# Fewer filler matmuls, a quartered first turn and an earlier weight load at the start of a fused Fourier filter and PReLU product kernel

## The chip, the cores and the metric

The kernel runs on one core of one Trainium2 chip. The metric is device microseconds of one execution; lower is better. The engines are TensorE (PE, whose weight loads are listed as PEld), VectorE (DVE), ScalarE (ACT), GpSimd (POOL) and SyncE (SP). SP and POOL issue the transfers.

## The reference

A Fourier filter along the sequence, then two products with a PReLU between them. There are 8 batches of 3008 tokens with 256 channels; the hidden width is 2048.

```python
def _attn_ref(x, filt_r, filt_i):
    X = np.fft.rfft(x, axis=1)
    F = (filt_r + 1j * filt_i)[None, :, :]
    Y = X * F
    return np.fft.irfft(Y, n=x.shape[1], axis=1).astype(np.float32)

def _moe_ref(x, w_in, w_out, alpha):
    h = x @ w_in
    g = np.maximum(h, 0.0) + alpha * np.minimum(h, 0.0)
    return (g @ w_out).astype(np.float32)
```

## The kernel before

The transform of length 3008 is split as 94 x 32. For a batch it has four steps on PE: a first stage of length 94 (`piece_a`), a stage of length 32 with twiddles (`piece_b`), the product with the filter on DVE, the inverse of length 32 (`piece_c`), and the inverse of length 94 (`inverse`, called by `half_d` and `pair_d`, L291), which leaves the filtered tokens transposed in `yT`. Between stages the data are turned. Batches 1 to 7 turn through DRAM while the products of earlier batches run. Batch 0 has nothing to hide behind, so class `First` turns it by matmuls with an identity.

After that the tokens go through in blocks of up to 512. A block's up-product (`up`, or `up4` for the very first block, L582) multiplies 16 slices of `w_in` with `yT`, ACT evicts, DVE computes the PReLU as g + min(g, 0) (alpha - 1), and the down-product (`down`, L613) multiplies with `w_out`. The first block's up-product is made in halves of 256 tokens: steps 0, 2, 4 and 6 take tokens 0 to 255, steps 8 to 14 the others. Work of the transforms is put between steps by hand with `put(step, ...)`. Every engine works its own list in the order in which the program wrote it.

What the change touches is all before step 2 of the first block:

- The first stage of batch 0 (loop at L459, pieces 0 to 7, two for each of the four loaded chunks of x). Between pieces `warm(n, ...)` (L455) puts n filler matmuls of 512 columns whose results nobody reads.
- The product loop (L493, kp = 0 to 11): `piece_b(kp + 2)` writes a product on DVE (L371), `piece_c(kp)` the inverse on PE (L392), `keep_c` the eviction. `piece_c` reads two tables, `twi_s` and its swapped copy `twx_s`; for kp = 4 to 7 the swapped copy is made by POOL (`swapped(8, nc.gpsimd)`, L445 and L446). At kp = 4 a memset on DVE (L497) and then the loads of `w_in` (L499), a chunk of x for batch 1, `w_out` (L502) and three more chunks of x are written into POOL's queue.
- The turn and the last stage of batch 0 (L519 to L524). `side_t(f)` turns the first four of 32 columns for channel half f, evicted by ACT for f = 0 and by DVE for f = 1. `half_t(2)` and `half_t(3)` turn two columns each of the next four. `half_d(0)` and `half_d(2)` make the last stage of the first 376 tokens for channel half 0 and 1.
- Step 0 evicts those two `half_t` and turns the PReLU slopes (`slopes`, L661 to L663); step 1 makes `half_d(1)` and `half_d(3)`, the next 376 tokens, and turns the next columns (`piece_t(2)`).

Accumulators: `bank("h")` takes one of two wide buffers (`psH`), `bank("f")` the single wide buffer `psF`, `bank("o")` one of two narrow ones (`psO`, 512 values). Buffers of a pool are used in turn, and a matmul into one waits for the eviction of what was in it.

Of the kernel before, what the change touches and what calls it, by code (L numbers as in the profile page):

```python
# [14 lines left out]
N1 = 94  # L15
# [40 lines left out]
def kernel(  # L56
# [10 lines left out]
    nc = tc.nc  # L67
# [37 lines left out]
    id16 = ids[:, 0:128]  # L105
# [4 lines left out]
    yT = konst.tile([128, 2, 2 * NFFT], FP16, name="yT")  # L110
# [5 lines left out]
    def load_x(b, c, held=False):  # L116
        xs = p_x.tile([128, 8 * D], FP16, name="xs")
        if held:
            for r in (slice(0, 32), slice(64, 96)):
                nc.vector.memset(xs[r, 0:2], 0.0)  # L120
        if b:
            for r in (slice(0, 48), slice(48, N1)):
                nc.gpsimd.dma_start(out=xs[r], in_=xrow(b, c)[r])  # L123
        else:
            w = 8 * D // (1 + (c == 3))
            for o in range(0, 8 * D, w):
                nc.gpsimd.dma_start(out=xs[0:N1, o : o + w], in_=xrow(b, c)[:, o : o + w])
        return xs
# [23 lines left out]
    def banks(wide):  # L152
        if wide:
            return psH.tile([128, 2, 512], FP32, name="hps")
        return psF.tile([128, 2, 512], FP32, name="psF")

    def bank(kind):
        if kind == "o":
            return psO.tile([128, 2, D], FP32, name="op").rearrange("p k d -> p (k d)")
        return banks(kind == "h")[:, 0]  # L160
# [151 lines left out]
    def on_act(o, i):  # L312
        nc.scalar.activation(o, i, AF.Copy)  # L313

    def on_dve(o, i):
        nc.vector.tensor_copy(o, i)  # L316

    both = (on_act, on_dve)


    class First(Fft):
# [86 lines left out]
                    nc.tensor.matmul(pt[0:96, u // 2, o : o + 128], m[:, f, n * i + u], id16,  # L408
                                     start=True, stop=True)

        def side_t(self, f):
            pt = bank("o")
            for u in range(4):
                nc.tensor.matmul(pt[0:96, 128 * u : 128 * u + 128],
                                 self.vm.rearrange("p (f s m) -> p f s m", f=2, m=96)[:, f, u], id16,
                                 start=True, stop=True)
            return self.zt[:, 0:4, 128 * f : 128 * f + 128], pt[0:96].rearrange("p (s d) -> p s d", s=4)

        def half_t(self, i, kind):
            pt = bank(kind).unsqueeze(1)  # L420
            self.turn(pt, i, 2)
            return self.zt[:, 2 * i : 2 * i + 2].rearrange("p a d -> p (a d)"), pt[0:96, 0]

        def piece_t(self, i, evict):
            pt = banks(False)
            self.turn(pt, i, 4)
            evict(self.zt[:, 4 * i : 4 * i + 4].rearrange("p (h a) d -> p h (a d)", h=2), pt[0:96])

    nc.sync.dma_start(out=ids, in_=id_d.ap())
    nc.vector.tensor_copy(signs_s, ids[:, 128:130])  # L430
# [2 lines left out]
    def table(ka, kb):  # L433
        nc.sync.dma_start(out=twf_s[:, ka:kb], in_=consts["twf"].ap()[:, ka:kb])

    def inverse_table(ka, pb):
        for i in range(4):
            nc.tensor.matmul(pb[:, 128 * i : 128 * i + 128],
                             twf_s[:, ka + 2 * i : ka + 2 * i + 2].rearrange("p k m -> p (k m)"), id16,
                             start=True, stop=True)  # L440
        on_act(twi_s[:, ka : ka + 8].rearrange("p k m -> p (k m)"), pb)

    def swapped(ka, eng):
        t, o = twi_s[:, ka : ka + 8], twx_s[:, ka : ka + 8]
        eng.tensor_scalar(o[:, :, 32:64], t[:, :, 0:32], gs_s, None, OP.mult)  # L445
        eng.tensor_scalar(o[:, :, 0:32], t[:, :, 32:64], gs_s, -1.0, OP.mult, OP.mult)  # L446

    xc = {(0, c): load_x(0, c) for c in range(4)}
    f0 = First()
# [3 lines left out]
    def warm(n, pw):  # L453
        for _ in range(n):
            nc.tensor.matmul(pw.rearrange("p (r c) -> p r c", r=4), id16,  # L455
                             id16.unsqueeze(1).to_broadcast([128, 4, 128]), start=True, stop=True)

    warm(10, bank("o"))
    for i in range(8):  # L459
        f0.piece_a(i, i % 3 < 2)  # L460
        if i == 3:
            inverse_table(0, bank("o"))
            swapped(0, nc.vector)
            warm(3, bank("o"))
        elif i % 2 == 1:
            warm((8, 0, 3, 0)[i // 2], bank("o"))
        if i in (5, 7):
            ka = 4 * i - 12
            nc.vector.memset(twf_s[:, ka : ka + 8, 0:1], 0.0)
            table(ka, ka + 8)  # L470
# [22 lines left out]
    for kp in range(12):  # L493
        if 0 < kp < 10:
            f0.piece_b(kp + 2)
        if kp == 4:
            nc.vector.memset(win_s[:, :, 0:1], 0.0)  # L497
            for kt in range(2):
                nc.gpsimd.dma_start(out=win_s[:, kt], in_=moe_w_in[kt * 128 : (kt + 1) * 128])  # L499
            xc[(1, 0)] = load_x(1, 0)  # L500
            for q in range(2):
                nc.gpsimd.dma_start(  # L502
                    out=wout_s[:, 8 * q : 8 * q + 8],
                    in_=moe_w_out[1024 * q : 1024 * q + 1024].rearrange("(j p) d -> p j d", p=128))
            for c in range(1, 4):
                xc[(1, c)] = load_x(1, c)
        f0.piece_c(kp)
        if kp > 9:
            f0.keep_c(kp, (on_act, on_act) if kp == 10 else both, 1)
        elif kp % 2 == 1:  # L510
            f0.keep_c(kp - 1, (on_act, on_act))
            if kp < 7:
                f0.turn_at(kp + 5, 2, on_act)
# [3 lines left out]
    for o in (32, 96):  # L517
        nc.gpsimd.dma_start(out=filt_s[o : o + 32], in_=filt_s[o - 32 : o])
    warm(3, bank("h"))  # L519
    on_act(*f0.side_t(0))  # L520
    on_dve(*f0.side_t(1))
    later = [f0.half_t(2, "h"), f0.half_t(3, "f")]
    f0.half_d(0, on_act, "o")
    f0.half_d(2, on_dve, "o")  # L524

    sizes = [512] * 5 + [384] + [512] * 6
    blocks = []
# [96 lines left out]
    def put(step, fn, *args):  # L624
        plan.setdefault(step, []).append((fn, args))
# [33 lines left out]
    def slopes():  # L659
# [2 lines left out]
        nc.vector.tensor_copy(al_s, alp[:, 0:16])  # L662
        nc.vector.tensor_scalar(alm_s, al_s, 1.0, -1.0, OP.mult, OP.add)  # L663

    put(1, f0.half_d, 1, on_act, "o")
    put(1, f0.half_d, 3, on_dve, "o")
    put(1, f0.piece_t, 2, on_dve)
# [22 lines left out]
    for b in range(3, NB):  # L690
        p = 96 * (b - 1)
# [20 lines left out]
    for step in range(16):  # L712
        if step % 2 == 0:
            blk.up4(step // 2 % 4, step // 8,
                    {0: [lambda: on_dve(*later[0]), lambda: on_act(*later[1]), slopes],
                     8: [lambda: f0.pair_d(3, on_dve)]}.get(step, []))
        for fn, args in plan.pop(step, ()):
            fn(*args)
# [4 lines left out]
    for p, t0, tn in blocks[1:]:  # L723
        blk = Block(p, t0, tn)
        for j in range(16):
            n = psum.get(step, 0)
# [50 lines left out]
```

## Time and profile before

| what | value |
|---|---|
| median of 3 runs | 769.6 us (769.01 to 769.75) |
| the profiled execution | 769.81 us, span 768.0 us |
| PE busy | 757.2 us (99% of the span) |
| DVE busy | 633.5 us (82%) |
| ACT busy | 582.8 us (76%) |
| POOL busy | 145.7 us (19%) |
| mean granted TensorE clock | 1.000 |

A stretch or a row gives its start and its length in microseconds from the span's start. In the timeline, brackets give the idle time of the engine before the row and what ended it. In the chain of waits each row is the work, the transfer or the wait that the next one had to wait for; "issue" is time in which nothing that the profile shows was waited for. In the table by stretches the columns are length, then busy time (and count) of PE, PEld, DVE, ACT and POOL, granted clock, the DMA engines' share and GB/s. Busy time of a matmul contains its passage through the array, so consecutive matmuls overlap.

### The profile page before, as it was taken

Reading aid. Unit: us, or ns where it says so; the run is one execution under the profiler, and the core shown is the slowest. Engines: PE = TensorE matmul, PEld = TensorE weight load, DVE = VectorE, ACT = ScalarE, POOL = GpSimd, SP = SyncE. Lnnn points to the kernel's source line nnn. Section 1 sums busy time; section 2 is a strip of 40 time slices with the busy share of each in tenths; the row PEclk is TensorE's granted clock in tenths of the full one; section 3 lists DMA queues with packets and bytes.
Section 4 is the critical chain, followed back from the end, with each engine's and each line's share of the span. In section 5 each row is a group of like instructions: output and inputs, shape, how many; then the busy total and the mean of one; then the engine's idle time right before and its main releaser. Section 6 shows DMA issues by size and latency. Waiting matters only on the chain.

```text
span 768.0 us, 16563 instructions
## 1 busy us (share of the span) xinstructions
PE 757.2 (99%) x6536; PEld 507.5 (66%) x6536; DVE 633.5 (82%) x1160; ACT 582.8 (76%) x670; POOL 145.7 (19%) x275
## 2 busy tenths in 40 slices
PE   8899999999999999999999999999999999999998
PEld 4666667666666666666666666766666666766666
DVE  4898975889889998899978998999877888666663
ACT  4787787888778787887778787787777777776664
POOL 6511560222211211121202222022101212000000
PEclk9999999999999999999999999999999999999999
DMA  9996796574853559533883538544453223510111
GB/s 163 168 237 166 148 200 200 155 175 128 189 144 78 137 136 199 147 93 95 186 212 87 134 94 180 177 93 118 129 158 92 71 68 96 152 36 28 42 42 56
DMA packets 97198, 100.04 MB, mean 130 GB/s; under 512 B 12054, under 2 KB 83366, under 8 KB 96928
## 3 DMA queue, kind: packets, MB, share of 16 engines
q1 hardware_dynamic: 82384, 69.50, 31.2%
q0 software_dynamic: 14736, 29.49, 21.3%
q8 instruction: 51, 0.84, 0.5%
q14 instruction: 27, 0.22, 0.1%
HBM read 55.02 MB, written 46.66 MB: 132 GB/s over the span
## 4 chain that ended last, share of the span: by engine, by line
PE 94%; DVE 2%; ACT 2%; DMA 1%; issue 0%; POOL 0%; ACTq 0%
PE op L613 42%; PE hps L559 41%; PE psF L291 3%; PE hps L269 2%; PE psF L238 1%; DMA win_s<-in_moe_w_in_dram 1%; PE op L455 1%; PE hps L184 1%; PE hps L210 1%; DVE gtb L596 1%; ACT asb L313 1%; DVE m L595 1%; PE hps L582 0%; ACT gtb L568 0%; DVE zt L316 0%
## 5 line engine op out<-in xcount | busy, mean ns | idle before, releaser
L568 ACT ACTIVATE gtb<-hps 128x1024 f16<-128x1024 f32 (+1 forms) x376 | 377.6, 1007 | 134.2 <-PE hps L559 131.1
L613 PE MATMUL op<-wout_s,gtb 128*128 128x256 f16 x3008 | 431.3, 273 | 0.0
L559 PE MATMUL hps<-yT,win_s 128*128 128x512 f16 (+1 forms) x1504 | 418.4, 375 | 0.9 <-ACT asb L313 0.3
L613 PEld LDWEIGHTS <-gtb 128*128 128x128 f16 x3008 | 290.8, 98 | 164.3 <-issue 10.7
L571 DVE TENSOR_SCALAR m<-gtb,alm_s 128x512 f16<-128x512 f16 (+1 forms) x752 | 227.0, 345 | 99.8 <-ACT gtb L568 98.3
L573 DVE TENSOR_TENSOR gtb<-gtb,m 128x2048 f16<-128x2048 f16 (+1 forms) x188 | 226.1, 1203 | 10.3
L559 PEld LDWEIGHTS <-win_s 128*128 128x128 f16 x1504 | 142.4, 98 | 55.2 <-issue 6.0
L252 POOL DMA_DIRECT2D sw<-ww x144 | 71.7, 506 | 414.5 <-DVE ww L245 408.7
L618 ACT ACTIVATE osb<-op 128x512 f32<-128x512 f32 (+1 forms) x97 | 56.6, 583 | 12.3 <-PE op L613 11.2
L313 ACT ACTIVATE asb<-hps 128x1024 f16<-128x1024 f32 (+1 forms) x56 | 56.6, 1019 | 5.6 <-PE hps L184 4.3
L313 ACT ACTIVATE v<-hps 128x1024 f16<-128x1024 f32 (+1 forms) x43 | 43.4, 1010 | 10.9 <-PE hps L269 10.6
L245 DVE TENSOR_TENSOR ww<-psF,filts_s 128x1024 f16<-128x1024 f32 x42 | 51.1, 1216 | 0.2 <-PE psF L238 0.2
L246 DVE TENSOR_TENSOR uu<-psF,filt_s 128x1024 f16<-128x1024 f32 x42 | 50.9, 1213 | 0.0
L313 ACT ACTIVATE yT<-psF 128x752 f16<-128x752 f32 x58 | 46.1, 795 | 2.0 <-PE psF L291 1.9
L291 PEld LDWEIGHTS <-zt 96*128 96x128 f16 x512 | 28.5, 98 | 6.8 <-issue 1.0
L291 PE MATMUL psF<-wi_s,zt 96*128 96x94 f16 x448 | 27.9, 205 | 0.1
L250 POOL DMA_DIRECT2D uu<-ww x24 | 19.7, 1232 | 31.8 <-DVE uu L246 23.8
L257 DVE TENSOR_TENSOR uu<-uu,sw 128x1024 f16<-128x1024 f16 x36 | 24.5, 681 | 0.3 <-DMA sw<-ww 0.3
L194 DVE TENSOR_TENSOR xs<-xs 47x2048 f16<-47x2048 f16 x16 | 19.5, 1219 | 0.4
L123 POOL DMA_DIRECT2D xs<-in_x_dram x24 | 17.5, 1012 | 12.2 <-PE hps L559 4.8
L198 DVE TENSOR_TENSOR xs<-xs 47x2048 f16<-47x2048 f16 x16 | 19.3, 1209 | 0.0
L269 PE MATMUL hps<-uu,twi_s 64*64 64x256 f16 x336 | 17.3, 281 | 0.0
(93 smaller groups left out, 261.5 us busy)
## 6 DMA issues: line engine op xcount, KB each, us to landing
out_dram<-osb SPq DMA_DIRECT2D x128, 128.0 KB
v_dram<-v SPq DMA_DIRECT2D x84, 128.0 KB
zt<-v_dram SPq DMA_DIRECT2D x28, 384.0 KB
sw<-ww POOLq DMA_DIRECT2D x144, 64.0 KB, 2.5
xs<-in_x_dram POOLq DMA_DIRECT2D x40, 192.0 KB, 6.3
at<-a_dram SPq DMA_DIRECT2D x40, 192.0 KB
a_dram<-asb SPq DMA_DIRECT2D x32, 192.0 KB
a_dram<-asb SPq DMA_DIRECT2D x12, 384.0 KB
```

The lines of the kernel that those rows point to most:

```text
L245: nc.vector.tensor_mul(ww, px, fs)
L246: nc.vector.tensor_mul(uu, px, f)
L252: nc.gpsimd.dma_start(out=sw[o : o + 32], in_=ww[i : i + 32])
L269: nc.tensor.matmul(ps[64 * par : 64 * par + 64, e, 256 * h : 256 * h + 256], twi_s[r, 4 * q + 2 * h + par], u[r, par, h], start=True, stop ...
L291: nc.tensor.matmul(ps[:, m], self.zt[:, 8 * g + 4 * mh + m, dh * 128 : dh * 128 + 128], self.wi, start=True, stop=True)
L313: nc.scalar.activation(o, i, AF.Copy)
L559: nc.tensor.matmul(self.hps[:, j % 2, 0:tn], win_s[:, kt, j * 128 : (j + 1) * 128], yT[:, kt, self.t0 : self.t0 + tn], start=(kt == 0), st ...
L568: nc.scalar.activation(g[:, 2 * i : 2 * i + 2], self.hps[:, :, 0:tn], AF.Copy)
L571: nc.vector.tensor_scalar(m[:, 2 * i + h], g[:, 2 * i + h], 0.0, a, OP.min, OP.mult)
L573: nc.vector.tensor_add(g, g, m)
L613: nc.tensor.matmul(self.op[:, si - s0], self.gts[k][:, 128 * si : 128 * si + 128], wout_s[:, k], start=(si == s0 and k == 0), stop=(si == ...
L618: nc.scalar.activation(osb[:, 0:m], self.op[:, 0:m], AF.Copy)
```

## The change

Four edits:

1. Fillers between first-stage pieces: 8, 0, 3, 0 after pieces 1, 3, 5, 7 become 4 after piece 1 and 1 after piece 5; the three after piece 3 stay.
2. `side_t` is replaced by `quarter_t(f, h, kind)`: two of the four columns each, h = 0 evicted by ACT and h = 1 by DVE, for f = 0 in narrow buffers and for f = 1 in wide ones. The next four columns are turned at once (`whole_t(1)`) into `psF` and evicted by DVE alone in step 0.
3. `half_d(0)` and `half_d(2)` are replaced by `first_d`, which makes only columns 0 to 63 of the last stage, which are tokens 0 to 255: channel half 0 in two parts of 32 columns (ACT and DVE), channel half 1 in one of 64 (ACT). The other 30 columns of both channel halves are made in step 1, in one narrow buffer evicted by ACT, ahead of `half_d(1)`.
4. The memset of `win_s` and the loads behind it move from kp = 4 to kp = 3.

```diff
-        def side_t(self, f):
-            pt = bank("o")
-            for u in range(4):
-                nc.tensor.matmul(pt[0:96, 128 * u : 128 * u + 128],
-                                 self.vm.rearrange("p (f s m) -> p f s m", f=2, m=96)[:, f, u], id16,
-                                 start=True, stop=True)
-            return self.zt[:, 0:4, 128 * f : 128 * f + 128], pt[0:96].rearrange("p (s d) -> p s d", s=4)
+        def quarter_t(self, f, h, kind):
+            pt = bank(kind)[0:96, 0:256].rearrange("p (s d) -> p s d", s=2)
+            for u in range(2):
+                nc.tensor.matmul(pt[:, u], self.vm.rearrange("p (f s m) -> p f s m", f=2, m=96)[:, f, 2 * h + u],
+                                 id16, start=True, stop=True)
+            return self.zt[:, 2 * h : 2 * h + 2, 128 * f : 128 * f + 128], pt
+
+        def first_d(self, dhs, x0, x1, kind):
+            n, w = len(dhs), x1 - x0
+            ps = bank(kind)[:, 0 : 4 * n * w].rearrange("p (a m x) -> p a m x", a=n, m=4)
+            for a, dh in enumerate(dhs):
+                for m in range(4):
+                    nc.tensor.matmul(ps[:, a, m], self.zt[:, m, 128 * dh : 128 * dh + 128], self.wi[:, x0:x1],
+                                     start=True, stop=True)
+            o = yT[:, dhs[0] : dhs[0] + n, 4 * x0 : 4 * x1]
+            return o.rearrange("p a (x m) -> p a x m", m=4), ps.rearrange("p a m x -> p a x m")
...
-        def piece_t(self, i, evict):
+        def whole_t(self, i):
             pt = banks(False)
             self.turn(pt, i, 4)
-            evict(self.zt[:, 4 * i : 4 * i + 4].rearrange("p (h a) d -> p h (a d)", h=2), pt[0:96])
+            return self.zt[:, 4 * i : 4 * i + 4].rearrange("p (h a) d -> p h (a d)", h=2), pt[0:96]
+
+        def piece_t(self, i, evict):
+            evict(*self.whole_t(i))
...
-        elif i % 2 == 1:
-            warm((8, 0, 3, 0)[i // 2], bank("o"))
+        elif i in (1, 5):
+            warm(4 if i == 1 else 1, bank("o"))
...
-        if kp == 4:
+        if kp == 3:
             nc.vector.memset(win_s[:, :, 0:1], 0.0)
...
     warm(3, bank("h"))
-    on_act(*f0.side_t(0))
-    on_dve(*f0.side_t(1))
-    later = [f0.half_t(2, "h"), f0.half_t(3, "f")]
-    f0.half_d(0, on_act, "o")
-    f0.half_d(2, on_dve, "o")
+    for f, kind in enumerate("oh"):
+        for h in range(2):
+            both[h](*f0.quarter_t(f, h, kind))
+    later = f0.whole_t(1)
+    on_act(*f0.first_d((0,), 0, 32, "o"))
+    on_dve(*f0.first_d((0,), 32, 64, "o"))
+    on_act(*f0.first_d((1,), 0, 64, "h"))
...
+    put(1, lambda: on_act(*f0.first_d((0, 1), 64, N1, "o")))
     put(1, f0.half_d, 1, on_act, "o")
...
-                    {0: [lambda: on_dve(*later[0]), lambda: on_act(*later[1]), slopes],
+                    {0: [lambda: on_dve(*later), slopes],
```

## The prediction

> **What bounds the kernel now.** I read the page's slices first, then the table by stretches, the chain of waits, and the timeline of the first 56 us, where every edit lies.
>
> ```profile
> PE   8899999999999999999999999999999999999998
> 56.00:256.00 200.00, 199.36 (x1636) 130.36 (x1633) 167.66 (x307) 160.13 (x182) 49.27 (x82) 1.00 0.65 160
> 256.00:456.00 200.00, 199.85 (x1687) 133.82 (x1686) 182.22 (x324) 159.04 (x182) 35.92 (x72) 1.00 0.54 134
> ```
>
> The second column of a stretch is PE's busy time: from 56 us on it idles 0.64 us, then 0.15 us, in 200. Nothing there is edited, so the change is worth what it moves the point at which this full stretch begins. Before it, by the chain:
>
> ```profile
> 24.41 0.43 POOL win_s L499
> 24.85 0.19 issue
> 25.03 8.59 DMA win_s<-in_moe_w_in_dram
> 33.62 0.05 issue
> 33.67 0.61 PE hps L582 x4
> ...
> 38.92 0.95 DVE yT L316
> ...
> 41.31 1.14 DVE m L595 x4
> ...
> 54.63 1.14 DVE zt L316
> 55.77 0.04 issue
> 55.82 0.49 PE psF L291 x8
> ```
>
> The second half of the first up-product (L582, kt = 1) waits for w_in until 33.67. PE then works without a gap to 39.82, its product at 38.39 releases DVE, and DVE is the chain from 40.45 to 55.77. So whatever is late at 35.32, where the second up-product starts, is late at 56. The edits act on two stretches ahead of it: first-stage pieces to products (6 to 30 us), and the turn (30 to 35).
>
> **The change, part by part.** All terms are against the profiled execution: span 768.0 us, 769.81 with what lies around it, 0.2 us above the median of 769.6 of three runs, so I add the difference to the median.
>
> *Fillers.* Six of 512 columns go: four after pieces 0 and 1, two after 4 and 5. Eight of them take 1.77 us in the chain, so 0.22 us each, 1.3 us off PE. Pieces 2 and 3 start at 9.85, their chunk has landed at 8.16 (trace's landings); they move up 0.88. The last half chunk lands at 11.89, so piece 7 (13.12) can move 1.0 at most; DVE casts without a gap from 12.29 to 14.35, and that row starts 0.85 sooner. So the first product (15.91) comes at about 15.05: its filter rows have landed at 14.72.
>
> What is late next is POOL.
>
> ```profile
> 22.33 0.49 POOL L446 TENSOR_SCALAR gtb<-twi_s,signs_s 128x256 f16<-128x256 f16 x1
> 22.55 0.10 PEld L392 LDWEIGHTS <-uu 64*128 64x128 f16 x2 [0.20 <-issue]
> 22.90 0.27 PEld L392 LDWEIGHTS <-uu 64*128 64x128 f16 x14 [0.25 <-issue]
> ```
>
> The fifth last-stage product (L392) stops after two matmuls until POOL has written its swapped table, 22.33 + 0.49 = 22.82. In the built order that matmul waits for POOL's semaphore. POOL's time doesn't depend on PE: it issues filter loads back to back from 18.77, which itself waited 0.37 us for a filter landing. So PE resumes at 22.9 as before, and from there to 25.33 it has no gap: the ninth product's input (L366, 24.45, 0.41 long) cannot be ready before 24.86, DVE follows 0.07 later (15.84 to 15.91 at the first), so at 24.93 instead of 25.15. Of 0.85 us, 0.22 is left. Bounds: the two table loads and five small ones on SP's queue, behind DVE's memsets, also go 0.85 sooner and share the DMA engines with the filter loads for which POOL waits; that could hold POOL up by one wait of the size seen (0.37), leaving -0.15. If POOL is somehow earlier, the next limit is the second third of the filter, landed at 19.78 for a product at 20.60: 0.75. I take 0.1, nearer the row.
>
> *Weights one product sooner.* The memset of w_in (0.06 us on DVE) stands behind the sixth product instead of the seventh, at about 22.1. POOL is free of its cast at 22.96, so it issues w_in there instead of at 24.41, and behind it, in unchanged order, the two loads of x, two of w_out and six more of x: all 1.44 sooner, past nothing else in POOL's queue. The second half lands at 33.62 less 1.44 if the engines give that time back; they are at 0.61 share in 24 to 28 us, and the two last table loads land only at 24.93, so I allow 0.2: 32.4. If the cover fails and only the idle share is won, (1 - 0.61) x 1.44 = 0.6: 33.0.
>
> *Quarters, and 256 tokens only.* Without a wait for weights, before: DVE's yT of the second half (32.64 + 0.55) would release kt = 1 at about 33.29. After, times before the 0.1 of the fillers: turning matmuls from 30.86, 0.056 apart; eviction starts 0.256 after the last matmul of its group (31.034 to 31.290). ACT's first quarter 31.18 to 31.57, DVE's 31.29 to 31.72, ACT's second 31.44 to 31.83, DVE's 31.64 to 32.06 (nearest rows: 256 wide, 0.384 on ACT, 0.425 on DVE, which overlap their successors by about 0.1). First-half products of 32 columns end for ACT at 32.15, for DVE at 32.32. The trace has no eviction of 128 values: between DVE's 16 wide copy (0.175) and its 256 wide cast (0.425); I take 0.29. So 32.61, and kt = 0 starts at 32.67, lasts four times 0.109, kt = 1 at 33.11; the second half (ACT, 256 wide) is ready at 32.87, w_in at 32.4, both hidden. 33.67 - 33.11 = 0.56 sooner, 0.66 with the fillers.
>
> *What is left over comes back behind it.* The remaining 30 columns of both halves become a new ACT eviction (240 values, between 0.384 for 256 and less; I take 0.37) and it stands behind the first activation of 1024 values:
>
> ```profile
> 34.37 1.02 ACT L590 ACTIVATE gtb<-hps 128x1024 f16<-128x1024 f32 x1 [1.09 <-issue]
> 35.29 0.48 ACT L313 ACTIVATE yT<-op 128x376 f16<-128x376 f32 x1
> ...
> 34.21 0.23 PE L661 MATMUL op<-id,al 16*128 16x16 f32 x1
> 34.37 0.66 PE L291 MATMUL op<-wif_s,zt 96*128 96x94 f16 x8
> 34.87 0.61 PE L408 MATMUL psF<-ids,v 128*96 128x128 f16 x8
> 35.32 1.04 PE L582 MATMUL hps<-yT,win_s 128*128 128x256 f16 x8
> ```
>
> Here PE runs from the up-product through both half products (L291) and the next turn to the second up-product, 33.67 to 35.32: 1.65 us. There are two small accumulator buffers ("o"). In the new sequence they go: slopes, the 30 columns, half product 1, half product 3. The last takes the buffer of the 30 columns, and the built order gives it a wait for ACT that it lacked. From the start of kt = 1: last matmul 0.33, activation starts 0.33 later, ACT's next 0.92 behind it (34.37 to 35.29), 0.37 for the eviction, 0.05 to the matmul, four matmuls 0.17, eight turns 0.45: 2.62. Behind the waiting matmul stand that turn and the second up-product, for which ACT, then DVE wait. Added: 2.62 - 1.65 = 0.97. Bounds: 0 if the eviction got ahead of the activation; 1.2 if it lasts as the 376 wide one (0.48) and the activation starts late as in the row at 36.39 plus 0.1. The single whole turn on DVE (1.21, for 0.68 there and 0.58 on ACT) ends at about 33.8, before half product 1 needs it at 34.1; it stays hidden.
>
> **Sum.** -0.56 - 0.1 + 0.97 = +0.3 us: 769.9.
>
> **Rivals.** (a) *The new wait costs nothing*: -0.66, 768.9; with the fillers' other bound of 0.75 in place of 0.1, 768.3. For: ACT has idle time at 34. Against: engines run in order and the eviction stands behind the activation. (b) *POOL doesn't hold the products*: +0.97 - 0.56 - 0.75 = -0.34, 769.3. (c) *The weights come no sooner*, because the transfers in front set their pace: kt = 1 at 33.67, +0.97, 770.6; for it, DMA engines at 1.08 share in 31 to 34; against, 0.61 in 24 to 28. (d) *The clock falls, slower*: the fillers keep TensorE fed while it waits for chunks. The first ten take 0.445 us each (4.45 in the chain), later ones 0.22, so PE starts at half rate, though the clock column says 1.00. If the gaps after 12.6 put it back for a stretch like the first one (2.5 to 8 us), half of 5.5 us of work is lost, 2.75, less PE's idle time there (0.16 + 0.3) and the 0.65 that POOL hides anyway: 1.6 on top of 0.3, 771.5. It decides from gaps longer than those that PE survives now, 0.72 us (29.09 to 29.81); I expect 0.2 to 0.6 us.
>
> The Trainium skill speaks on (d): "TensorE: Matmul & The Clock Gate", part 1, has the clock fall back after an idle window of about 3.4 us. The doubling of the fillers' rate agrees with its two states; that gaps of 0.72 us leave the rate alone agrees too, so by its rule (d) would not happen here.
>
> **Chances.** The forecast 0.42, (a) 0.18, (b) 0.12, (c) 0.11, (d) 0.10, something unseen 0.07. About 0.2%, 1.54 us, is what a measurement of this kernel can tell: faster means under 768.06, reached only by a third of (a) and a bit of the unseen: 0.07. Slower is over 771.14: (d), a quarter of (c) with the upper bound of the wait, and half of the unseen: 0.16. Within: 0.77. The range 768.5 to 771.2 takes in (a), (b), (c) and the unknown costs, and leaves out most of (d). The forecast's own range is 769.4 to 770.6.
>
> **What would show it.** Right: first product (DVE, filter row) at about 15.1, but the twelfth ending within 0.3 of 29.76; PE stopping at 22.9 for POOL; w_in's issue near 23.0 and no wait of L582's successor for it; kt = 1 near 33.0; the 240 wide eviction behind the first activation, an idle PE of about 0.8 us before the second half product, and the second up-product at 35.5 to 35.8. Wrong: that product before 35.2, the products' end before 29.3, or matmul durations doubled after 9 us. The forecast fails as a whole if the start of the full stretch at 56 doesn't carry over to the end.

## The result and the profile after

The changed kernel takes 771.74 us (median of 12 executions, 770.12 to 775.3); beside it on the same chip the kernel before takes 769.68 us (12 executions, 768.98 to 771.3). The ratio is 1.003 with an interval of 1.0016 to 1.0043: slower by 0.3%, where 769.9 was predicted and 771.2 was the upper end of the range.

The profiled execution took 772.23 us, 2.42 us more than that of before. The first view is its chain of waits (start, length, work).

```profile
12.32 1.53 POOL filt_s L147 x3
13.85 2.79 DMA filt_s<-in_filt_i_dram
16.64 1.23 DVE uu L371
...
30.91 1.40 PE hps L467 x3
32.30 0.43 PE op L414 x4
...
34.70 1.05 PE hps L596 x8
...
35.82 0.72 ACT gtb L604
36.54 0.20 issue
36.74 0.37 ACT yT L313
...
57.05 1.14 DVE zt L316
58.19 0.04 issue
58.23 0.49 PE psF L291 x8
```

The full stretch begins at 58.23 instead of 55.82, so all of the loss, 2.41 us, arises in the edited part. Two things in this chain were not in that of before. Loads of the filter (filt_s) hold DVE until 16.64. (The chain infers which load it was and names one issued at 13.85. The last load of the rows that this product reads is the one issued at 12.32; it landed at 16.21, and the product starts 0.42 us behind it, as it does 0.41 behind the same load in e1 and e5.) And the three fillers ahead of the turn (L467) take 1.40 us in the chain. From the first of them to the turn it is 1.25 us (30.84 to 32.09), where the same three took 0.71 in the trace of before (30.15 to 30.86): TensorE works at about half its rate. The table by stretches, in the columns explained with the profile before, has the clock; first the kernel before, then the changed one.

```profile
16.00:20.00 4.00, 3.54 (x107) 2.49 (x104) 4.00 (x4) 3.01 (x4) 3.55 (x8) 1.00 1.11 169
28.00:31.00 3.00, 2.05 (x63) 1.25 (x55) 2.18 (x3) 2.02 (x5) 2.08 (x4) 1.00 1.04 201
31.00:34.00 3.00, 2.51 (x31) 1.81 (x30) 1.83 (x3) 1.56 (x3) 0.10 (x1) 1.00 1.08 199
```

```profile
16.00:20.00 4.00, 2.40 (x77) 1.64 (x78) 3.37 (x3) 2.00 (x4) 3.49 (x8) 1.00 1.07 151
28.00:31.00 3.00, 2.13 (x80) 1.51 (x80) 2.35 (x4) 1.17 (x3) 1.51 (x3) 0.95 1.05 205
31.00:34.00 3.00, 3.00 (x25) 2.21 (x24) 1.22 (x3) 1.50 (x5) 0.81 (x2) 0.50 1.15 196
56.00:256.00 200.00, 199.20 (x1635) 130.28 (x1634) 168.23 (x307) 160.02 (x183) 47.61 (x79) 1.00 0.65 158
```

From 16 to 20 us PE is busy for 2.40 us instead of 3.54: this is the wait for the filter. From 31 to 34 the granted clock (third column from the end) is 0.50, and PE is busy throughout. The clock's own records put the half rate at 30.70 to 34.11 us, 3.41 us long. Over a span of 770 us one such stretch lowers the mean clock by 0.5 x 3.41 / 770 = 0.002, so the mean clock of an execution tells how many it had: 1.000 none, about 0.998 one, 0.996 two. (A last 0.001 more or less is the clock falling behind the last matmul, a little before the span ends; e12's fell at 767.19 of 767.81 us.) Of the 12 executions after, 2 had none (770.12 and 770.21), 6 had about one (median 771.6), 4 had two (median 773.6). The kernel before is not free of it: in the three groups in which it ran beside the experiments, 16 of 35, 15 of 35 and 17 of 33 executions were at 0.998 or less, and those at 1.000 had medians of 769.74, 770.04 and 769.50, those at 0.998 of 771.33, 771.12 and 770.90. One stretch costs it 1.1 to 1.6 us.

Why the filter came late shows in the timeline (start, length, engine, line, work, count, idle before). Before:

```profile
13.22 0.07 DVE L469 MEMSET twf_s<- 128x8 f16 x1
13.31 1.42 SPq L434 DMA_DIRECT2D twf_s<-c_twf  x2
15.91 2.35 DVE L371 TENSOR_TENSOR uu<-hps,filt_s 128x1024 f16<-128x1024 f32 x2 [0.21 <-DMA filt_s<-in_filt_r_dram]
```

After:

```profile
11.93 0.07 DVE L481 MEMSET twf_s<- 128x8 f16 x1
12.02 1.57 SPq L446 DMA_DIRECT2D twf_s<-c_twf  x2
12.32 0.49 POOL L147 DMA_DIRECT2D filt_s<-in_filt_i_dram  x1 [0.56 <-DMA xs<-in_x_dram]
16.63 2.36 DVE L371 TENSOR_TENSOR uu<-hps,filt_s 128x1024 f16<-128x1024 f32 x2 [2.08 <-DMA filt_s<-in_filt_i_dram]
17.91 0.30 PE L366 MATMUL hps<-at,twf_s 64*32 64x256 f16 x8 [1.44 <-DVE uu L371]
```

DVE's memset of the table twf_s comes 1.29 us sooner, because the casts ahead of it follow the first-stage pieces. SP's load of that table waits for the memset and is now issued at 12.02, ahead of the filter load that POOL issues at 12.32; before, it was issued at 13.31, behind the same filter load (12.17). By the landings in the trace this filter load landed at 14.72 before and lands at 16.21 after. DVE then idles 2.08 us and PE 1.44.

All fourteen profiles, those of the experiments below included, order themselves this way. In the six with few fillers and the tables not held back (after, e1, e6, e10, e11, e12) the table load is issued 0.02 to 0.35 us ahead of the filter load, which lands 3.5 to 4.0 us after its own issue. In the other eight it is issued 0.3 to 1.5 us behind, and the filter load lands 2.5 to 2.9 us after its issue.

Some 0.4 of the 1.29 us is not the fillers' doing. TensorE starts at half rate, and in the profiled execution its clock first rose at 6.81 us, in that of before at 8.20, so pieces 0 and 1 took 0.69 us instead of 1.28. In e10, where it rose at 8.03, the table load is issued at 12.42, 0.89 sooner than before, and still just ahead of the filter load (12.44).

### The profile page after: what moved, and what is told of

It reads as the page before. It is cut to its first block, busy times and chain, and to the rows that moved or that the text cites. A ratio compares the mean times of both kernels' runs of the same rounds, so it can differ in the third digit from the quotient of the medians.

```text
span 770.5 us, 16579 instructions
## 1 busy us (share of the span) xinstructions
PE 757.1 (98%) x6542; PEld 507.6 (66%) x6542; DVE 633.8 (82%) x1161; ACT 582.7 (76%) x672; POOL 145.1 (19%) x275
## 4 chain that ended last, share of the span: by engine, by line
PE 92%; DVE 3%; DMA 2%; ACT 2%; issue 1%; POOL 0%; ACTq 0%; POOLq 0%
PE op L627 42%; PE hps L573 41%; PE psF L291 3%; PE hps L269 2%; PE psF L238 1%; DMA xs<-in_x_dram 1%; PE hps L210 1%; PE hps L184 1%; DMA out_dram<-osb 1%; DVE gtb L610 1%; ACT asb L313 1%; DVE m L609 1%; DVE uu L371 1%; PE hps L596 0%; ACT gtb L582 0%
```

## Experiments

Each ran beside the kernel before on the same chip, in three groups; 770.23, 770.25 and 770.38 us are the medians of before in these groups. "Under full clock" counts executions with a mean clock of 0.998 or less.

| kernel | median us (executions) | ratio to before, interval | under full clock | median at 1.000 |
|---|---|---|---|---|
| e1_fillers | 772.14 (12) | 1.0020 (1.0009 to 1.0031) | 12 | none |
| e2_quarters | 771.54 (12) | 1.0008 (0.9996 to 1.0019) | 8 | 770.39 |
| e3_weights | 769.73 (12) | 0.9992 (0.9979 to 1.0005) | 4 | 769.38 |
| e4_no_fill | 770.53 (12) | 1.0002 (0.9990 to 1.0015) | 5 | 770.00 |
| before, these rounds | 770.23 (35) | | 16 | 769.74 |
| e5_hold | 772.13 (12) | 1.0023 (1.0012 to 1.0034) | 8 | 770.53 |
| e6_cover | 770.91 (11) | 1.0007 (0.9998 to 1.0015) | 0 | 770.91 |
| e7_weights_cover | 769.97 (11) | 0.9996 (0.9988 to 1.0005) | 0 | 769.97 |
| e8_no_stall | 769.87 (11) | 0.9996 (0.9986 to 1.0007) | 2 | 769.80 |
| before, these rounds | 770.25 (35) | | 15 | 770.04 |
| e9_best | 769.50 (11) | 0.9998 (0.9990 to 1.0007) | 1 | 769.44 |
| e10_head | 771.81 (11) | 1.0017 (1.0008 to 1.0026) | 7 | 771.04 |
| e11_tail | 772.63 (11) | 1.0030 (1.0014 to 1.0047) | 8 | 770.54 |
| e12_fill_cover | 770.46 (11) | 1.0001 (0.9992 to 1.0010) | 0 | 770.48 |
| before, these rounds | 770.38 (33) | | 17 | 769.50 |

### One edit at a time: e1 to e4

e1_fillers is the kernel before with the first edit alone.

```diff
-        elif i % 2 == 1:
-            warm((8, 0, 3, 0)[i // 2], bank("o"))
+        elif i in (1, 5):
+            warm(4 if i == 1 else 1, bank("o"))
```

> The kernel before with the fewer fillers alone. Theory 1 (loads and clock): DVE's memsets come sooner, so SP's table load of the second third overtakes the last load of the first filter third; the first product starts near 16.6 us instead of 15.9, PE stands still behind it for over 1 us, and the granted clock falls for a 3.4 us stretch in most executions: about 771.3 us, mean clock mostly 0.996 to 0.998. Theory 2 (the turn): the loss sits in the new turn and its wait, fewer fillers cost nothing: 769.5 to 769.9, clock 1.000.

The filler edit by itself makes the kernel slower by 0.2%, and every one of its 12 executions is under full clock. Its first product comes at 16.42 us instead of 15.91, and the same filter rows land at 16.01. So the loss needs neither the quarters nor the weights.

e2_quarters is the changed kernel with the old fillers and the weights where they were.

```diff
-        elif i in (1, 5):
-            warm(4 if i == 1 else 1, bank("o"))
+        elif i % 2 == 1:
+            warm((8, 0, 3, 0)[i // 2], bank("o"))
...
-        if kp == 3:
+        if kp == 4:
```

> The kernel before with the quartered turn and the last stage for 256 tokens alone. Theory 1: the first product stays at 15.9, the clock at 1.000, and only the new wait for ACT shows, 0.2 to 0.5 us: about 770.0. Theory 2: the turn holds PE up and the clock falls there: about 771.3.

Its timeline shows the two waits of the prediction one after the other:

```profile
33.98 0.61 PE L596 MATMUL hps<-yT,win_s 128*128 128x256 f16 x4 [0.53 <-DMA win_s<-in_moe_w_in_dram]
...
36.02 0.42 PE L291 MATMUL op<-wif_s,zt 96*128 96x94 f16 x4 [0.67 <-ACT yT L313]
```

Quarters without the earlier weights win nothing, because kt = 1 waits for w_in, and the wait for ACT is added behind it. In this execution the clock was at half from 36.12 to 39.53, after a stretch with both waits in it.

e3_weights is the kernel before with the fourth edit alone.

```diff
-        if kp == 4:
+        if kp == 3:
```

> The kernel before with the weights one product sooner alone. Both theories: w_in is issued near 23.2 us, lands near 32.4, and the second half of the first up-product starts at about 33.3 instead of 33.67; the second up-product follows as much sooner: about 769.3, clock 1.000.

At full clock it takes 0.36 us less than before at full clock (769.38 against 769.74); 4 of its 12 executions are under full clock, where none was expected. The second half of the first up-product starts at 33.31 instead of 33.67, at once behind the first half: the wait for w_in is gone, and the yield is what was free there.

e4_no_fill is the changed kernel with the old fillers.

```diff
-        elif i in (1, 5):
-            warm(4 if i == 1 else 1, bank("o"))
+        elif i % 2 == 1:
+            warm((8, 0, 3, 0)[i // 2], bank("o"))
```

> The changed kernel with the old number of fillers, the other edits kept. Theory 1: first product at 15.9, clock 1.000 in nearly all executions, and what is left is the wait for ACT less the weights' gain: +0.2 to +0.5 us, about 770.0. Theory 2: as slow as the changed kernel, about 771.5.

At full clock it takes 770.00, 0.26 more than before. 5 of 12 executions are under full clock, as often as with the kernel before. Its profiled execution, at full clock, shows the forecast's two main steps in the timeline:

```profile
15.39 3.49 DVE L371 TENSOR_TENSOR uu<-hps,filt_s 128x1024 f16<-128x1024 f32 x3 [0.21 <-PE hps L366]
...
22.34 0.48 POOL L458 TENSOR_SCALAR gtb<-twi_s,signs_s 128x256 f16<-128x256 f16 x1
22.88 0.26 PEld L392 LDWEIGHTS <-uu 64*128 64x128 f16 x13 [0.40 <-issue]
...
33.48 1.02 ACT L604 ACTIVATE gtb<-hps 128x1024 f16<-128x1024 f32 x1 [0.96 <-PE hps L596]
34.40 0.74 ACT L313 ACTIVATE yT<-op 128x240 f16<-128x240 f32 x2
34.82 0.33 PE L291 MATMUL op<-wif_s,zt 96*128 96x94 f16 x4 [0.67 <-ACT yT L313]
...
35.43 1.04 PE L596 MATMUL hps<-yT,win_s 128*128 128x256 f16 x8
```

Its first product is 0.52 us sooner than that of before though no filler is gone: its clock rose at 6.98 us instead of 8.20, and pieces 0 and 1 took 0.75 us instead of 1.28. PE still stops until POOL has written the swapped table, 22.34 + 0.48 = 22.82, and resumes at 22.88; the twelfth product ends only 0.23 sooner. The eviction of the 30 columns stands behind the activation of 1024 values, PE idles 0.67 us for it, and the second up-product starts 2.64 us behind kt = 1 (32.79).

### What brings the clock down: e5, e6, e10, e11, e12

e5_hold is the changed kernel with the table loads held back, so that they can't overtake the filter.

```diff
-        if i in (5, 7):
-            ka = 4 * i - 12
-            nc.vector.memset(twf_s[:, ka : ka + 8, 0:1], 0.0)
-            table(ka, ka + 8)
+        if i == 7:
+            nc.vector.memset(twf_s[:, 8:16, 0:1], 0.0)
+            table(8, 16)
...
     f0.turn_at(1, 1, on_dve, True)
+    nc.vector.memset(twf_s[:, 16:24, 0:1], 0.0)
+    table(16, 24)
```

> The changed kernel with the two table loads held back to where they were (the first memset after piece 7, the second after DVE's cast of the first turn), fillers still few. Theory 1a (the overtaking makes the late product): the filter's first third lands near 14.8 us again, the first product starts at 15.0 to 15.4, the twelfth ends by 29.6, PE's idle 1.4 us before the third product's input is gone; the clock falls about as often as in the kernel before (half of the executions), median about 770.4, executions at clock 1.000 about 769.9. Rival 1b (the loads are late because of the x chunks, or the clock falls for want of the fillers themselves): product still near 16.5, or every execution below clock 1.000, about 771.7.

```profile
13.54 1.67 SPq L446 DMA_DIRECT2D twf_s<-c_twf  x2
15.46 3.71 DVE L371 TENSOR_TENSOR uu<-hps,filt_s 128x1024 f16<-128x1024 f32 x3 [0.60 <-DMA filt_s<-in_filt_r_dram]
17.14 0.40 PE L450 MATMUL op<-ids,twf_s 128*128 128x128 f16 x4 [1.28 <-DMA twf_s<-c_twf]
```

This confirms the overtaking: with the table issued at 13.54 the filter lands at 15.05 and the first product comes at 15.46, 1.17 sooner than in the changed kernel. But the time stays, and 8 of 12 executions are still under full clock, so neither expectation was met. The last row says why this can't tell what the late filter costs: PE now idles 1.28 us for the table that was held back, about as long as it idled for the filter (1.44). The wait was moved, not taken away.

The next kernel puts fillers into PE's waits instead. e6_cover adds them to the changed kernel in three places: around the inverse table (14 to 18 us), between the last products (26 to 31 us), and in the wait for ACT.

```diff
+    warm(2, bank("o"))
     inverse_table(8, bank("o"))
+    warm(6, bank("o"))
...
+        if kp in (8, 10, 11):
+            warm({8: 2, 10: 1, 11: 3}[kp], bank("h" if kp == 11 else "f"))
         f0.piece_c(kp)
...
+    put(1, lambda: warm(3, bank("h")))
     put(1, f0.half_d, 3, on_dve, "o")
```

> The changed kernel with fillers put into PE's waits: 2 and 6 around the second table, 2, 1 and 3 before the products of kp = 8, 10 and 11, 3 before the half product that waits for ACT; all else, the late filter too, as in the changed kernel. If the falling clock makes most of the loss: clock 1.000 in nearly all executions and about 770.2, the time of the changed kernel's two executions at clock 1.000. If the clock is only a sign and the late loads make the loss: about 771.7 still.

No execution is under full clock, though the profiled one has its first product as late as 17.52. The median is 770.91, where 770.2 was expected. More work on PE, with none of the change undone, takes the ratio to before from 1.0030 (1.0016 to 1.0043) to 1.0007 (0.9998 to 1.0015). What is left against before at full clock is 0.87 us.

e10_head has only the first of the three groups, e11_tail only the second, both on the changed kernel; e12_fill_cover has the first two on the kernel before with the first edit alone.

```diff
+    warm(2, bank("o"))
     inverse_table(8, bank("o"))
+    warm(6, bank("o"))
```

```diff
+        if kp in (8, 10, 11):
+            warm({8: 2, 10: 1, 11: 3}[kp], bank("h" if kp == 11 else "f"))
```

> The changed kernel with fillers only in the waits ahead of the first products (2 and 6 around the second table, 14 to 18 us), none later. If the hole behind the late filter makes the surplus of falls over the kernel before: clock below 1.000 in about half of the executions, never two stretches, median about 771.0. If the fewer matmuls between the pieces let it fall earlier, or the turn does: as the changed kernel, 771.7, most executions below 1.000.

> The changed kernel with fillers only in the waits of kp = 8, 10 and 11, none ahead of the first products. If the hole at 14 to 18 us is deep enough by itself: clock below 1.000 in most executions, one stretch (0.998), 771.0 to 771.7. If only the waits at 26 to 30 us matter: clock 1.000 in nearly all, about 770.4.

> The kernel before with the fewer fillers, and fillers in PE's waits (2 and 6 around the second table, 2, 1 and 3 before kp = 8, 10 and 11). The clock stays at 1.000, so what is left is the price of the late filter alone: 0.4 to 0.8 us above the executions of the kernel before at clock 1.000, 770.4 to 770.8. If the late filter costs nothing (POOL's table holds the products anyway): 769.9 to 770.1.

With one group alone 7 and 8 of 11 executions are under full clock; with both, none in e6 (which has the third group besides) and none in e12. So there are two places, each deep enough by itself. (e10 never had two falls, as expected, but its median, 771.81, is that of the changed kernel and not 771.0.) Where the first is left open, the clock can fall there; the table by stretches of e11:

```profile
16.00:20.00 4.00, 1.92 (x38) 1.14 (x30) 2.81 (x3) 1.27 (x2) 3.76 (x8) 0.79 1.03 140
20.00:24.00 4.00, 3.87 (x124) 2.56 (x123) 3.22 (x4) 3.05 (x5) 3.29 (x8) 0.79 0.98 147
```

Here the clock is at half from 18.29 to 21.70, behind the wait for the filter. With e12, which is e1 plus fillers, 12 of 12 become 0 of 11, and the ratio goes from 1.0020 to 1.0001; 770.48 at full clock is still 0.98 us over before at full clock, where 0.4 to 0.8 was expected. The late filter is a part of that: the first product lies between 16.23 (e12's profile) and 17.52 (e6's) over the profiles of kernels with the first edit and without e5's hold. How the rest divides between it and the added fillers isn't separated: e12's profiled execution, 769.61, is its quickest.

### Looking for a better version: e7 to e9

e7_weights_cover is e3 with e6's fillers between the last products. e8_no_stall is e4 with the same fillers and with the 30 columns moved from step 1 to step 5, behind the work that PE had to wait with. e9_best is e8 with two fillers each ahead of products 8 and 10 only, and none ahead of product 11. The edits of e8 and e9 against e4:

```diff
+        if kp in (8, 10, 11):
+            warm({8: 2, 10: 1, 11: 3}[kp], bank("h" if kp == 11 else "f"))
...
-    put(1, lambda: on_act(*f0.first_d((0, 1), 64, N1, "o")))
+    put(5, lambda: on_act(*f0.first_d((0, 1), 64, N1, "o")))
```

```diff
+        if kp in (8, 10):
+            warm(2, bank("f"))
```

> The kernel before with the weights one product sooner and fillers in the waits of kp = 8, 10 and 11 (2, 1 and 3). If those waits are what lets the clock fall in half of the executions of the kernel before: clock 1.000 in nearly all, about 769.4, faster than before by 0.8. If not: 769.7 with the clock as mixed as with the weights alone.

> The changed kernel with the old fillers, the fillers of kp = 8, 10 and 11, and the 30 remaining columns made in step 5 instead of step 1, so that the half product doesn't stand behind ACT's first activation. If that wait costs the 0.97 us of the sum: second up-product at 34.6 to 34.9, clock 1.000, about 769.1. If the wait is hidden by something else (DVE's whole turn, the slopes): about 769.9, as the executions at clock 1.000 with the wait in.

> The changed kernel with the old fillers between the pieces, 2 fillers each before the products of kp = 8 and 10, and the 30 columns in step 5. Theory 1 (the waits of PE set the clock; weights and quarters gain, the wait for ACT takes it back): clock 1.000 in nearly all executions, first up-product's second half at 32.8 to 33.1, the second up-product 1.65 behind it, about 0.6 us under the executions of the kernel before at clock 1.000 and 0.9 under its median. If the wait for ACT was not what stood in the way: no better than the changed kernel with the old fillers at clock 1.000, 0.3 above the kernel before.

e7's fillers remove the clock's falls (before: 15 of 35, here 0 of 11), but three of them ahead of the twelfth product delay it: the second up-product starts at 35.11, where e3 had 34.95. In e8 and e9 the added wait is gone. The timeline of e9:

```profile
34.72 0.48 ACT L313 ACTIVATE yT<-op 128x376 f16<-128x376 f32 x1
34.75 1.04 PE L598 MATMUL hps<-yT,win_s 128*128 128x256 f16 x8
```

Behind the activation stands no eviction of the 30 columns, and the second up-product starts at 34.75, 1.64 us behind kt = 1 (33.11), 0.57 sooner than before. 1 of 11 executions is under full clock, against 17 of 33. The median is 0.9 us below that of before on the same chip, the lowest of all versions; but at full clock it is 769.44 against 769.50, and the ratio is 0.9998 with an interval that contains 1. That e9 is faster than before isn't shown.

## Why the prediction was wrong

The points of time in the two profiles, step by step, against the forecast:

| from | to | before | after | difference | predicted |
|---|---|---|---|---|---|
| start | twelfth product's matmuls | 29.81 | 30.37 | +0.56 | -0.1 |
| those | turn's first matmul | 1.05 | 1.72 | +0.67 | 0 |
| that | kt = 1 | 2.81 | 3.04 | +0.23 | -0.56 |
| kt = 1 | second up-product | 1.65 | 2.64 | +0.99 | +0.97 |
| sum | | 35.32 | 37.77 | +2.45 | +0.3 |

Two steps failed.

*The larger is the falling clock*, for which the sum has no term: rows two and three, 0.67 and 0.79 us off, 1.46 of the 2.15 us between forecast and profile. That these rows are the clock shows in profiles of the same work at full clock: e4, e5 and e10 take 1.05 us in row two, and 2.16 or 2.17 in row three, against 1.72 and 3.04.

The prediction had it as rival (d), with a chance of 0.10 and 771.5 us, and made it hang on gaps: "It decides from gaps longer than those that PE survives now, 0.72 us". Gaps aren't what decides. For each trace I worked out the share of time in which columns stream through TensorE (each matmul's columns at 0.42 ns, matmuls that run side by side counted once; fillers of 512 columns issue 0.216 us apart at full clock), in stretches of 3.41 us on the grid that the clock's first rise fixes. Here are two of these stretches, each with the one that follows it, first of e5, then of the changed kernel:

```profile
15.24:18.65 3.41, 2.13 (x65) 1.34 (x62) 3.06 (x3) 1.81 (x3) 3.08 (x7) 1.00 1.03 169
18.65:22.07 3.42, 3.33 (x121) 2.33 (x112) 3.03 (x4) 3.18 (x5) 3.01 (x7) 1.00 1.16 171
```

```profile
27.29:30.70 3.41, 2.11 (x88) 1.52 (x80) 3.02 (x3) 1.52 (x4) 2.04 (x4) 1.00 1.04 203
30.70:34.11 3.41, 3.41 (x41) 2.50 (x34) 1.27 (x3) 1.80 (x6) 1.10 (x3) 0.50 1.14 195
```

In e5's PE waits 1.28 us in one piece (ahead of 17.14), columns stream for 0.43 of the time, and the clock stays at 1.00 in the next stretch. In the changed kernel's the longest wait is 0.55 us (ahead of 29.41), shorter than the 0.72 that "PE survives now", and PE is busy for 0.62 of the time, as in e5; but columns stream for only 0.36, and the clock falls. The four falls seen in profiles before 40 us followed stretches with 0.36 (after), 0.40 (e1), 0.35 (e2) and 0.30 (e11). These are the four lowest of all such stretches in the fourteen profiles; the lowest without a fall had 0.43 (e1 and e5) and 0.45 (e1 and after). PE's busy share doesn't separate them: a stretch with 0.70 was followed by a fall (e1), one with 0.63 wasn't (e5). So what decides is how much streams in a whole stretch, with a limit between 0.40 and 0.43 by this measure.

The grid lies elsewhere in every execution: the first rise was at 8.20 us before, at 6.81 after, between 5.40 and 8.41 in the experiments. So I shifted the grid over each trace and counted the positions that have a stretch under the limit, once with 0.40 and once with 0.43:

| kernel | positions with a stretch under the limit | executions under full clock |
|---|---|---|
| after | 0.95 to 1.00 | 10 of 12 |
| e1 | 0.70 to 0.93 | 12 of 12 |
| e11 | 0.69 to 0.81 | 8 of 11 |
| e2 | 0.58 to 0.72 | 8 of 12 |
| e5 | 0.27 to 0.61 | 8 of 12 |
| before | 0.29 to 0.39 | 16 of 35, 15 of 35, 17 of 33 |
| e10 | 0.28 to 0.45 | 7 of 11 |
| e4 | 0.23 to 0.38 | 5 of 12 |
| e3 | 0.22 to 0.28 | 4 of 12 |
| e8, e9 | 0.00 to 0.01 | 3 of 22 |
| e6, e7, e12 | 0.00 | 0 of 33 |

This is why before falls in about half of its executions, and why one profile at full clock gave no warning.

That the price of (d) is near the measured median is partly luck. It has one stretch of 5.5 us at half rate somewhere behind 12.6 us, and no late filter; what came was one or two stretches of 3.41 us, in the profile at 30.70, and a late filter besides.

*The smaller step that failed* is in the fillers: "So the first product (15.91) comes at about 15.05: its filter rows have landed at 14.72." The landing was taken from the trace of before and held fixed. The prediction did see that SP's table loads move 0.85 us forward "and share the DMA engines with the filter loads for which POOL waits", but priced that only for POOL's wait. The filter load for which DVE waits was the next one behind them, and it landed 1.49 us later. That is the first row of the table: +0.56 instead of -0.1.

The Trainium skill has a sentence for this: "DMA: Bandwidth & Descriptors", section "Issuing engines are not separate DMA queues", has transfers of different engines run on the same DMA engines and interleave. The 1.49 us here, and their return in e5, agree with it.

The rule that the prediction quoted from the Trainium skill ("TensorE: Matmul & The Clock Gate", part 1) has the right length of the stretch, 3413 ns, running freely, which every fall here agrees with: the four lie 7, 7, 9 and 3 such lengths behind the clock's first rise, to 0.01 us (after, e1, e2, e11). That the fall needs an idle window is what the runs contradict. The same page's section "A second HAM failure mode: psum-queue depth-cycling" tells of a clock that oscillates under frequent short idle times; it names no amount, and it is the sentence that would have spoken for rival (d).

*Right were*: the cap by POOL's table (e4: start 0.52 sooner, twelfth product 0.23); the new wait for ACT, 2.64 us against 2.62 in the sum; the turn in quarters (e4: kt = 1 at 2.16 us behind the turn's first matmul instead of 2.81, so -0.65 for -0.56); the weights' landing, 32.33 us for 32.4, though the number is luck: behind the late products they were issued at 23.83 and not near 23.0, and in e4, where they were issued at 22.92, they landed at 31.82; the widths of the new evictions (0.28 to 0.29 for 128 values, 0.37 for 240); and that whatever is late at the second up-product is late at 56 us and at the end (+2.45, +2.41 and +2.42). e4 at full clock, which has these terms without the two failed steps, lies 0.26 us over before, for the sum's -0.56 + 0.97 = +0.41. The changed kernel's own two executions at full clock, 770.12 and 770.21, lie about 0.5 over the 769.7 of before, near the forecast's +0.3. That doesn't show the sum right: they are two, the clocks of the 769.7 are not on record, and the other kernels with a late filter (e6, e10, e11, e12) lie 0.9 to 1.5 over before at full clock.

*What stays open*: what the late filter costs by itself at full clock, since e5 put another wait in its place and the other kernels with it have added fillers or few executions at full clock. And the exact measure of activity: the share of streaming orders the kernels rightly at both ends, but e5, e10 and before fall more often than their one trace gives, and e8 and e9 fell in 3 of 22 executions where theirs give next to none. No profile of these fallen executions was taken.

## What to carry to other kernels

Fillers do two things: they keep the clock up, and they time everything that waits behind the pieces they stand between; taking some away moves memsets, and with them the order in which transfers of different queues are issued, so each landing that a step relies on must be worked out anew. Before a stretch with many short waits is thinned out, count what streams through TensorE in any 3.4 us of it, and compare the mean clock of a dozen executions rather than of one. An eviction put behind a long one on the same engine makes whoever needs its buffer wait for both: here, behind an activation of 1.02 us, it cost 0.99 us at the second up-product, and none of that when it was made four steps later (e8 and e9).

## What was unexpected in the hardware

The clock fell to half with PE busy 0.62 of the preceding 3.41 us and no wait in it longer than 0.55 us, while a wait of 1.28 us inside one such stretch of e5 left it alone; what separates them is that columns streamed for 0.36 of the one and for 0.43 of the other. Adding matmuls whose results nobody reads made a kernel quicker (after to e6: ratio to before 1.0030 to 1.0007). A table load on one queue that was issued 0.30 us ahead of a filter load on another, instead of 1.14 us behind it, went with that load landing 3.89 us after its issue instead of 2.55.
